# Moving three transposing transfers, one key part and two hand-over no-ops in a hand-written instruction order

## The chip, the core and the metric

The kernel runs on one core of a Trainium2 chip. Times are device microseconds (us) of one execution. Its engines are named as in the profile: PE (TensorE matmul; PEld is its weight load), DVE (VectorE), ACT (ScalarE), POOL (GpSimd) and SP (SyncE, which here only issues transfers). POOLq, SPq and so on are the instruction queues of these engines, in which waits and issues of transfers stand.

## The reference

One input `x` of 2048 tokens by 448 features feeds two branches, which are combined by a gate:

```python
xn = layernorm(x)
# A: attention over a dilated window, 16 heads of 28
idx = pos[:, None] - 2 * arange(8)[None, :]        # 8 keys, every second token back
logits = einsum("bhsd,bhswd->bhsw", q, k[idx]) * 28 ** -0.5   # masked where idx < 0
s = einsum("bhsw,bhswd->bhsd", softmax(logits), v[idx]) @ wo
# B: feed-forward 448 -> 1792 -> 448
f = gelu(xn @ w1 + b1) @ w2 + b2
return x + s * silu(f)
```

## The kernel before

**Tiling.** The even and the odd tokens are taken apart, since the window only reaches tokens of the same parity; the 2048 positions are then 16 tiles of 128, numbered 0 to 15, and four chunks of four tiles. The features lie on the partitions in three full groups of 128 and a rest of 64.

**Stages.** Each tile is normalised and transposed (`xnT`). Projections give queries and keys (`qk_rows`, evacuated by ACT or DVE to `qk_tok` or `qk_pair`, and transposed by a transfer on SP into `qkT`) and values (`vproj`, evacuated to `v_tok`, written by a transfer on POOL to a DRAM tensor `v_rows`, and read back shifted by other transfers on POOL into `v`, `values`). Attention works on nine blocks of 224 to 228 positions, 0 to 8, each in two halves. For a block, `keys` makes two masked copies of its keys, `kb` (part 0 and part 1, each of two instructions); `scores` multiplies keys and queries (L680); ACT takes the exponential into `E` (L686); DVE or POOL multiplies by the mask (L696); `values_sum` multiplies by the values (L711); DVE divides into a buffer `a` (L722, L727), of which there are three in turn; and two transfers per half, on POOL or SP, write `a` to a DRAM tensor `o_rows` (L734). `turn` reads two tiles of `o_rows` back transposed (transfers on SP into `xnT`, whose earlier content is spent, or `oT`) and `final_pair` or `final` projects them (L745, L760). The feed-forward branch is `ff1` (L554, evacuated by ACT, L558) and `ff2` (L580, L606). `store` multiplies by the gate, adds `x` and writes out (L780).

**Row pairs.** Most projections run as a `pair`: two products of 64 rows each side by side in the array. A pair has two parts on PE, and between them a no-op on some other engine (L437): it waits for the last matmuls of the first part, and the second part waits for it. POOL, SP or ACT may carry the no-op.

**What sets the order.** Nothing is scheduled by a cost: a string `ORDER` lists all 1033 steps, and each engine executes its own steps in that order. A letter gives the engine (P = PE, V = DVE, A = ACT, G = POOL, S = SP, D = the landing of a transfer, which costs nothing by itself) and the number the step. A step can wait for another engine, and what stands behind it on its engine then waits too. Banks of PSUM and buffers are handed out in the same order.

The steps that the change and the prediction speak of:

| step | what it is |
|---|---|
| S449, S426, S442 | transposes of queries and keys of tiles 15, 13 and 14 (L300, `qkT<-qk_tok`, `qkT<-qk_pair`) |
| S375 | the same for tile 11, ahead of them on SP |
| S930, S932 | read-back of output rows, tiles 4 and 5, and 6 and 7 (L300, `xnT<-o_rows`) |
| S790, S797, S829, G788 | writes of `a` to `o_rows` (L734) of blocks 4 and 5 |
| G386, G390, G388, G392 | reads of `v` for block 4 (L294): two of 63 rows, then two of 64 |
| P783, P792 | first and second half of `values_sum` of block 4 (L711) |
| V861, A862 | the two key parts of block 7 (L665 on DVE, L663 on ACT) |
| P863, P868 | scores of block 7 (L680) |
| A891, A892, P893 | key parts and scores of block 8 |
| P964, P975 | final projections that read what S930 brings (L745) |
| 539, 514 | no-ops between the parts of two `ff1` pairs: P538 to P540, and P513 to P515 |
| A52 | a load of ACT's function table for gelu (L340) |
| V824 | the `a` of block 5's second half (L727), which reuses the buffer that S790 and G788 empty |
| P523 | first part of an `ff1` pair, whose bank V824 frees |

Of the kernel before, what the change touches and what calls it, by code (L numbers as in the profile page):

```python
# [39 lines left out]
V592 V745 V747 P732 V602 P377 V733 A603 V734 P370 G378 V735 P379 V736 G371 P354 V599 G739 S737 D738 D740 A383 S928  # L40
D929 V771 A600 P753 G384 D385 P372 V754 G355 V380 P356 A373 V755 G381 D382 P428 A357 V772 A360 P444 G358 D359 V756
V757 G361 D362 P773 V374 S445 S758 D759 P446 G429 G760 D761 G386 D387 A774 V750 S375 D376 P778 A776 V447 P430 A779
V752 P421 V801 A781 P762 V775 A448 G422 G390 D391 P423 V763 A431 V764 S449 D450 P451 G388 D389 A434 V765 V766 P605
A425 V424 G452 S767 D768 G392 D393 V777 G394 D395 V802 G396 D397 V604 G432 D433 S426 D427 V601 G435 D436 P453 V780
G606 P437 V782 G769 D770 A457 V454 P803 G458 D459 V831 A438 P439 A804 G455 D456 V832 P783 A806 P607 G805 V784 A441
V785 V786 V787 G461 D462 G463 D464 V440 S790 G788 D789 D791 V807 S442 D443 G460 P808 V611 P538 A809 V608 A811 P792
S539 P813 V810 A52 G465 D466 P513 V793 V794 G467 D468 P540 V795 S514 V796 A609 P515 V814 G799 S797 D798 D800 V815 A542
S932 D933 S930 D931 P528 V816 A541 V817 P533 V812 A516 A529 G818 D819 V610 G820 D821 P822 A612 P530 V861 A534 G469
D470 A517 V823 P535 V824 G471 D472 A532 P508 V825 V826 A537 V613 P523 G827 D828 S829 D830 A531 G509 A536 P510 S524
A862 P518 P953 S519 A512 P525 G954 A511 S934 D935 P955 A526 P520 V956 A527 P942 V960 G957 A522 V961 P833 P838 A521  # L50
G943 S958 D959 P944 S962 D963 A53 P614 V945 V949 V950 A839 S951 D952 A841 V840 V946 A834 P863 V842 S947 D948 G615 P868
A836 V835 P616 A869 V837 A871 G870 A864 A866 V865 G872 A891 P843 V620 P623 G867 V844 V845 A621 V846 A892 V847 V617
G848 D849 V622 P852 G850 D851 A618 S624 P893 P625 V853 A894 V854 A896 V855 V856 V619 G857 D858 V895 G859 D860 V897
P548 V629 V626 P964 A630 G549 A627 V631 P898 G965 P975 A899 V628 A901 P966 V900 G976 A54 V902 P543 S936 D937 V971 P977
# [68 lines left out]
def kernel(  # L123
# [16 lines left out]
    NT = S // P  # L140
# [7 lines left out]
    TPC = CH // P  # L148
# [236 lines left out]
    def norm(t):  # L385
        def f1(k):
            nc.vector.tensor_scalar(buf(p_xn, k)[:, :D], x_sb[:, t, :], mv[:, t, 0:1], rstd[:, t:t + 1],  # L387
                                    op0=ALU.subtract, op1=ALU.mult)
        a = plan.add("DVE", f1, [t_rs[t]], take=(p_xn,))

        def f2(_):
            nc.vector.tensor_copy(buf(p_xn, a)[:, D:], buf(p_xn, a)[:, KF:D])
        twice = plan.add("DVE", f2, [a])
        if t >= TPC:
            t_xT[t] = dma_T(xnT[:, :, t * P:(t + 1) * P], lambda: buf(p_xn, a)[:], [twice], (p_xn, a, 0))
            return
        halves, apart = [], t < 2
        for i in range(2):
            def f3(k, i=i):
                xn, tp = buf(p_xn, a), half_bank(buf(p_b, k if apart else (halves or [k])[0]))  # L400
                for kt in (2 * i, 2 * i + 1):
                    nc.tensor.transpose(tp[:, kt, :], xn[:, kt * P:(kt + 1) * P], ident[:])
            halves.append(plan.add("PE", f3, [twice if i else a, t_ident] + halves, take=() if i and not apart else (p_b,), give=((p_xn, a, 0),) if i else ()))

        n = 2 if t < 2 else 4
        copied = []
        for k0 in range(0, KT, n):
            def f4(k, k0=k0, b=halves[k0 // 2 if apart else 0]):
                copy(k.on, xnT[:, k0:k0 + n, t * P:(t + 1) * P], half_bank(buf(p_b, b))[:, k0:k0 + n, :])
            b = halves[k0 // 2 if apart else 0]  # L410
            copied.append(plan.add(("DVE", "ACT"), f4, [halves[(k0 + n - 1) // 2]], give=((p_b, b, 0),)))
        t_xT01[t], t_xT[t] = copied[0], plan.add("DMA", None, copied)
# [38 lines left out]
    def first_batch(tiles, tiles0=0):  # L451

        f = []
        for kt in range(3):
            for i, js in enumerate(tiles):
                def f1(k, kt=kt, i=i, js=js):
                    for q, j in enumerate(js):
                        j.part(buf(p_b, f[i] if kt else k, q), kt, 2, kt == 0, False)
                f.append(plan.add("PE", f1, ([t_xT01[tiles0 + i]] if kt < 2 else js[0].deps[:1]) + t_w[kt] + f[i:i + 1] * (kt > 0) + f[:1] * (i > 0), take=() if kt else (p_b,) * len(js) ))
        every = [(i, q, j) for i, js in enumerate(tiles) for q, j in enumerate(js)]  # L460

        def f2(k):
            def part(i, q, half):
                return lambda: tiles[i][q].part(buf(p_b, f[i], q), 3, half, False, True)
            together([part(0, 0, 0), part(1, 0, 0), part(0, 2, 0)], [part(0, 1, 1), part(1, 1, 1), part(1, 2, 1)])
        tt = plan.add("PE", f2, f + t_w[3])
        for i, q, j in every:
            j.evac(tt, f[i], q)

    t_row, t_qk = [[] for _ in range(NT)], {}  # L470

    def qk_rows(t, which):
        cs = slice(t * P, (t + 1) * P)

        def part(ps, kt, half, start, stop):
            r = half_rows(half)
            w = w_in[r, kt, which * D:(which + 1) * D] if kt < 3 else w_in3[r, 0, :]
            return nc.tensor.matmul(ps[:, :D], xnT[r, kt, cs], w, start=start, stop=stop)  # L478

        def evac(a, own, i):  # L480
            b = qk_tok[qk_at[t]]
            free = t_qk.get(max([u for u in range(t) if qk_at[u] == qk_at[t]], default=None))

            def fn(k):
                copy(k.on, b[:, which, :, :DH], buf(p_b, own, i)[:, :D].rearrange("p (h c) -> p h c", h=H))
            t_row[t].append(plan.add(("ACT", "DVE"), fn, [a, t_qz[qk_at[t]], free], give=((p_b, own, i),)))
            if len(t_row[t]) == 2:
                t_qk[t] = dma_T(qkT[:, :, :, cs].rearrange("p w g c -> p (w g) c"), lambda: b[:].rearrange("p w h c -> p (w h c)"),
                                t_row[t], None)
        return _Job(D, part, [t_xT[t]] + t_w[0] + t_w[1] + t_w[2], evac, (), t_w[3])  # L490

    t_v, v_at, h_at = {}, {}, {}
    t_vt = {}

    def vproj(t):
        k0 = t * P

        def part(ps, kt, half, start, stop):
            r = half_rows(half)
            w = w_in[r, kt, 2 * D:] if kt < 3 else w_in3[r, 1, :]  # L500
            return nc.tensor.matmul(ps[:, :D], xnT[r, kt, k0:k0 + P], w, start=start, stop=stop)  # L501

        def evac(a, own, i):
            b = v_tok[t % len(v_tok)]

            def fn(k):
                copy(k.on, b[:, :, :DH].rearrange("p (e x) c -> p e x c", e=2),
                     buf(p_b, own, i)[:, :D].rearrange("p (x e c) -> p e x c", e=2, c=DH))
            d = plan.add(("ACT", "DVE"), fn, [a] + t_vw + [t_vt[u] for u in (t - len(v_tok),) if u >= 0], give=((p_b, own, i),))
            t_vt[t] = dma_sb(lambda k: v_rows[k0:k0 + P, :], lambda: b[:].rearrange("p h c -> p (h c)"), [d])[1]  # L510
        return _Job(D, part, [t_xT[t]] + t_w[0] + t_w[1] + t_w[2], evac, (), t_w[3])
# [313 lines left out]
    def project(c):  # L825
        for t in range(c * TPC, (c + 1) * TPC):
            norm(t)
        vs = [vproj(t) for t in range(c * TPC, (c + 1) * TPC)]
        for i, t in enumerate((c * TPC, c * TPC + 2)):
            js = [[qk_rows(u, w) for w in range(2)] for u in (t, t + 1)]  # L830
            if not c and not i:
                first_batch([js[n] + [vs[n]] for n in range(2)], t)
            else:
                for n in range(2):
                    pair(*js[n], c < 2)
                pair(vs[2 * i], vs[2 * i + 1], c < 2)
        if c == NCH - 1:
            done = [j for t in range(c * TPC, NT) for j in (t_qk[t], t_vt[t])]
            t = plan.add("POOL", None, done)
            t.slots[p_g] = list(range(4, 4 + len(late_g)))  # L840
            t.give = tuple((p_g, t, i) for i in range(len(late_g)))
        for b in blocks_of[c]:
            values(b)

    project(0)

    def f_b1(k):
        nc.tensor.transpose(half_bank(buf(p_b, k))[:, 0, :], b1r[:], ident[:])
    b1_at = plan.add("PE", f_b1, [t_b1r, t_ident], take=(p_b,))
    t_b1 = plan.add("DVE", lambda _: nc.vector.tensor_copy(b1[:], half_bank(buf(p_b, b1_at))[:, 0, :NMT]), [b1_at], give=((p_b, b1_at, 0),))  # L850

    project(1)

    turned = [t_xT[t].deps[0] for t in range(TPC, 2 * TPC)]
# [43 lines left out]
    t = plan.add("POOL", None, [seen[b, 1][0] for b in range(2)])  # L898
# [43 lines left out]
```

## Time and profile before

| | |
|---|---|
| median of three runs | 152.55 us |
| the three runs | 151.75, 152.55 and 156.65 us |
| the profiled execution, its own time | 151.89 us |
| its span, first to last instruction | 150.2 us |
| PE, busy share of the span | 144.2 us, 96% |
| DVE | 109.8 us, 73% |
| ACT | 88.3 us, 59% |
| POOL | 64.0 us, 43% |
| granted TensorE clock | 0.999 |

Between the span and the execution's own time lie 1.7 us before the first and behind the last instruction. A busy share is an average over the whole span; what an edit is worth is read from the stretch in which it lies, here the one from about 75 to 120 us after the start.

### The profile page before, as it was taken

How to read it: one execution, taken by the hardware profiler on the slowest of the kernel's cores; microseconds unless marked ns; L12 is line 12 of the kernel's file. 1: busy time of each engine (PE TensorE's matmuls, PEld its weight loads, DVE VectorE, ACT ScalarE, POOL GpSimd, SP SyncE). 2: the span in 40 equal slices, each digit the busy share in tenths (PEclk: the TensorE clock that was granted, in tenths of full speed). 3: DMA queues.
4: the chain of work that ended last, by engine and by line, in shares of the span. 5: the costliest groups of instructions: out<-in, count | busy, mean ns of one | idle time of the engine just before them, and what ended most of it. 6: DMA issues, size and time to landing. Idle time of an engine off the chain costs nothing.

```text
span 150.2 us, 4657 instructions
## 1 busy us (share of the span) xinstructions
PE 144.2 (96%) x1828; PEld 79.9 (53%) x1828; DVE 109.8 (73%) x295; ACT 88.3 (59%) x161; POOL 64.0 (43%) x120
## 2 busy tenths in 40 slices
PE   7999999999999999999999699999999999999991
PEld 2444555444455665565565365556666664455570
DVE  3889944197954899989999689808689997581642
ACT  3253576776683772744673519989883976571120
POOL 6733594004535585741468457902363024110200
PEclk9999999999999999999999999999999999999999
DMA  4999998999499969998399899795102332264202
GB/s 145 303 273 321 207 199 190 243 311 258 116 138 203 117 152 225 230 209 179 109 223 178 98 244 175 189 194 137 65 0 73 76 101 62 71 155 112 65 31 61
DMA packets 43966, 24.17 MB, mean 161 GB/s; under 512 B 33822, under 2 KB 42022, under 8 KB 43944
## 3 DMA queue, kind: packets, MB, share of 16 engines
q1 hardware_dynamic: 41080, 17.25, 59.8%
q0 software_dynamic: 2720, 6.51, 16.4%
q8 instruction: 14, 0.23, 0.6%
q10 hardware_dynamic: 144, 0.11, 0.3%
q14 instruction: 8, 0.07, 0.1%
HBM read 9.70 MB, written 6.29 MB: 106 GB/s over the span
## 4 chain that ended last, share of the span: by engine, by line
PE 79%; DVE 8%; DMA 7%; issue 2%; SPq 2%; ACT 1%; DVEq 0%; POOLq 0%
PE bank L554 28%; PE bank L580 14%; PE bank L478 9%; PE bank L606 7%; PE bank L745 6%; DMA v<-v_rows 5%; PE bank L501 5%; PE bank L264 3%; DMA o_rows<-a 3%; PE bank L680 2%; PE bank L711 2%; DVE a L727 2%; SPq L300 2%; PE bank L760 1%; DVE E L696 1%
## 5 line engine op out<-in xcount | busy, mean ns | idle before, releaser
L554 PE MATMUL bank<-xnT,w 64*128 64x512 bf16 x392 | 46.9, 376 | 0.0
L558 ACT ACTIVATE h<-bank,b 128x512 bf16<-128x512 f32 x56 | 35.1, 685 | 15.7 <-PE bank L554 15.2
L580 PE MATMUL bank<-w,h 64*128 64x448 bf16 x336 | 33.8, 349 | 0.0
L554 PEld LDWEIGHTS <-w 64*128 64x128 bf16 x392 | 20.8, 94 | 18.7 <-issue 0.7
L478 PE MATMUL bank<-w_in,xnT 64*128 64x448 bf16 (+1 forms) x212 | 26.4, 351 | 0.2 <-DVE xnT L251 0.2
L686 ACT ACTIVATE E<-bank 128x456 bf16<-128x456 f32 (+1 forms) x36 | 17.4, 551 | 11.9 <-PE bank L680 10.8
L580 PEld LDWEIGHTS <-h 64*128 64x128 bf16 x336 | 17.4, 94 | 12.7
L727 DVE TENSOR_TENSOR a<-bank,rd 114x448 bf16<-114x448 f32 (+1 forms) x36 | 22.3, 623 | 1.6 <-DMA o_rows<-a 0.6
L734 POOL DMA_DIRECT2D o_rows<-a x25 | 13.3, 534 | 21.2 <-DVE a L727 9.4
L294 POOL DMA_DIRECT2D v<-v_rows x22 | 13.9, 635 | 8.6 <-PE bank L478 2.9
L478 PEld LDWEIGHTS <-xnT 64*128 64x128 bf16 (+1 forms) x212 | 10.4, 94 | 9.3 <-DVE xnT L251 0.7
L353 DVE BATCH_NORM_STATS2 st<-x_sb 128x6 f32<-128x448 bf16 x16 | 9.4, 610 | 6.9 <-DMA x_sb<-in_A_x_dram 6.8
L501 PE MATMUL bank<-w_in,xnT 64*128 64x448 bf16 (+1 forms) x106 | 13.7, 349 | 0.0
L622 DVE TENSOR_TENSOR y<-bank,b 128x448 f32<-128x448 f32 x15 | 9.0, 619 | 6.3 <-PE bank L606 5.0
L294 POOL DMA_DIRECT2D v_rows<-v_tok x16 | 9.1, 572 | 8.0 <-DVE v_tok L251 4.5
L634 ACT ACTIVATE t<-y 128x448 f32<-128x448 f32 x12 | 6.9, 580 | 8.0 <-DVE y L622 8.0
L606 PE MATMUL bank<-w,h 128*128 128x448 bf16 (+2 forms) x70 | 11.4, 315 | 0.0
L665 DVE TENSOR_SCALAR kb<-qkT,plane 128x512 bf16<-128x512 bf16 x30 | 10.5, 403 | 1.2 <-DMA qkT<-qk_tok 1.2
L696 POOL TENSOR_TENSOR E<-E,m_gen 128x456 bf16<-128x456 bf16 x8 | 8.5, 1076 | 6.7 <-ACT E L686 6.7
L776 POOL TENSOR_TENSOR o<-x_sb,sg 128x448 bf16<-128x448 bf16 x3 | 3.1, 1030 | 18.0 <-DVE sg L770 9.3
L387 DVE TENSOR_SCALAR xn<-x_sb,mv,rstd 128x448 bf16<-128x448 bf16 x16 | 6.2, 394 | 5.7 <-DMA xnT<-xn 3.4
L696 DVE TENSOR_TENSOR E<-E,m_gen 128x456 bf16<-128x456 bf16 (+1 forms) x24 | 9.0, 391 | 1.4 <-ACT E L686 1.4
(83 smaller groups left out, 181.1 us busy)
## 6 DMA issues: line engine op xcount, KB each, us to landing
v_rows<-v_tok POOLq DMA_DIRECT2D x16, 128.0 KB, 3.7
v<-v_rows POOLq DMA_DIRECT2D x14, 128.0 KB, 3.8
out_dram<-o SPq DMA_DIRECT2D x15, 112.0 KB, 1.7
w<-in_B_w_dram SPq DMA_DIRECT2D x2, 784.0 KB
o_rows<-a POOLq DMA_DIRECT2D x23, 64.1 KB, 2.9
w<-in_B_w_dram SPq DMA_DIRECT2D x2, 672.0 KB
x_sb<-in_A_x_dram SPq DMA_DIRECT2D x3, 448.0 KB, 7.3
w_in<-in_A_wqkv_dram SPq DMA_DIRECT2D x3, 336.0 KB, 5.1
```

Of the source, the lines that this page charges most:

```text
L294: nc.gpsimd.dma_start(dst(k), src())
L478: return nc.tensor.matmul(ps[:, :D], xnT[r, kt, cs], w, start=start, stop=stop)
L501: return nc.tensor.matmul(ps[:, :D], xnT[r, kt, k0:k0 + P], w, start=start, stop=stop)
L554: return nc.tensor.matmul(ps[:], w1[r, kt, ms], xnT[r, kt, cs], start=start, stop=stop)
L558: nc.scalar.activation(buf(p_h, own, i)[:], buf(p_b, own, i)[:], ACT.Gelu_apprx_tanh, bias=b1[:, mt:mt + 1])
L580: return nc.tensor.matmul(ps[:, :D], buf(*h_at[(c, mt)])[r, j * P:(j + 1) * P], w2[r, mt, :], start=start, stop=stop)
L606: nc.tensor.matmul(ps[:, :n], buf(*h_at[(c, mt)])[:, j * P:(j + 1) * P], w2[:, mt, cs], start=(mt == 0 and not biased), stop=(mt == NMT - 1))
L665: nc.vector.tensor_scalar(dst, src, plane[:, e:e + 1], None, op0=ALU.mult)
L686: nc.scalar.activation(buf(p_E, k)[:, :n], buf(p_b, a, r)[:, :n], ACT.Exp, scale=SCALE)
L696: (nc.gpsimd if k.on == "POOL" else nc.vector).tensor_tensor(out=E, in0=E, in1=m, op=ALU.mult)
L727: nc.vector.tensor_tensor(out=o, in0=sums(k, e)[:, :, :, :DH], in1=buf(p_rd, rd)[rows].unsqueeze(2).unsqueeze(3).to_broadcast((2 * nq, 8, ...
L734: (nc.gpsimd if k.on == "POOL" else nc.sync).dma_start(o_rows[n + i * nq:n + i * nq + nq, :], buf(p_a, own)[i * nq:i * nq + nq, i, :])
```

## The change

Nothing is added to the work or taken from it. In `ORDER`, with the rest of the string in place:

- S449 (and its landing D450) goes from before the second value projection of tiles 12 and 13 to behind S932, where S930 stood.
- S426 (D427) goes from ahead of S790 to just behind it.
- S930 (D931) goes from behind S932 to behind four output writes.
- V861 goes from behind V610 and P822 to behind V613, five DVE steps later.
- The no-ops 539 and 514 are issued by ACT and not by SP: 539 in front of A52, 514 behind it.

The step G460 in `project` is a bookkeeping step without an instruction: it hands the memory of the input weights on to the gate's buffers. It listed the landing of the query and key transposes among what must stand ahead of it in the string; two of these now stand behind it, so it lists the evacuations instead.

```diff
-V752 P421 ... A434 V765 V766 P605 ... S449 D450 P451 ...
+V752 P421 ... P451 ...
-... G432 D433 S426 D427 V601 ...
+... G432 D433 V601 ...
-... S790 G788 D789 D791 ... P538 A809 V608 A811 P792
-S539 P813 ... V795 S514 V796 ... S932 D933 S930 D931 P528
+... S790 S426 D427 G788 D789 D791 ... P538 A809 V608 A811 A539 P792 P813
+... V795 A514 V796 ... S932 D933
+S449 D450 P528
-... P530 V861 A534 ... V613 P523
+... P530 A534 ... V613 V861 P523
-... S947 D948
+... S947 S930 D931 D948
@@
-            done = [j for t in range(c * TPC, NT) for j in (t_qk[t], t_vt[t])]
+            done = [j for t in range(c * TPC, NT) for j in t_row[t] + [t_vt[t]]]
```

On SP, in the second half of the program, the rows stood as follows. `qk_tok_153` belongs to tile 11 (S375), `qk_tok_151` to tile 15 (S449), the first `qk_pair` to tile 13 (S426), the second to tile 14 (S442); the two `xnT<-o_rows` are S932 and S930.

```order
L300 DMA_TRANSPOSE qkT<-qk_tok_153 128x8x128
L300 DMA_TRANSPOSE qkT<-qk_tok_151 128x8x128
L734 DMA o_rows<-a 57x576
L300 DMA_TRANSPOSE qkT<-qk_pair 128x8x128
L734 DMA o_rows<-a 56x576
L300 DMA_TRANSPOSE qkT<-qk_pair 128x8x128
L734 DMA o_rows<-a 56x576
L300 DMA_TRANSPOSE xnT<-o_rows 128x4x256 x2
L734 DMA o_rows<-a 57x576
L300 DMA_TRANSPOSE oT<-o_rows 128x4x256
```

In the changed program the same stretch of SP reads:

```order
L300 DMA_TRANSPOSE qkT<-qk_tok_153 128x8x128
L734 DMA o_rows<-a 57x576
L734 DMA o_rows<-a 56x576
L300 DMA_TRANSPOSE qkT<-qk_pair 128x8x128 x2
L734 DMA o_rows<-a 56x576
L300 DMA_TRANSPOSE xnT<-o_rows 128x4x256
L300 DMA_TRANSPOSE qkT<-qk_tok_151 128x8x128
L734 DMA o_rows<-a 57x576
L300 DMA_TRANSPOSE oT<-o_rows 128x4x256
```

Between tile 11's transpose and the write S790 (the `56x576` row that comes first) stood two transposes, and now stands none; tiles 13 and 14 follow S790 back to back; tile 15 has S930's old place. S930 itself comes four output writes later, outside these rows.

On ACT, around the table load that leads from the exponentials of block 5 to the gelus of `ff1`, the difference is (+ now, - before; `PE_49` is PE's semaphore):

```order
 L686 ACTIVATE E<-bank_157 128x456 [waits PE_49]
 L686 ACTIVATE E<-bank_158 128x456 [waits PE_49]
-L340 ACT_TABLE_LOAD
+L340 ACT_TABLE_LOAD [waits PE_49]
 L340 ACTIVATE sink<-eps_t 128x1
-L634 ACTIVATE t_107<-y_104 128x448 [waits DVE_49]
+L634 ACTIVATE t_107<-y_104 128x448 [waits PE_49,DVE_49]
 L558 ACTIVATE h_128<-bank_156,b_71 128x512 [waits PE_49]
```

The two new waits are those of the no-ops, which have no row of their own: the table load now waits for the first part of one `ff1` pair (P538), and the tanh behind it for that of another (P513).

On DVE the key part V861 (`kb_149`) moves behind block 5's last divisions and a gate step:

```order
 L696 TENSOR_TENSOR E<-E,m_gen 128x456
 L638 SCALAR_TENSOR_TENSOR qkT<-t_107,y_104 128x448
-L665 TENSOR_SCALAR kb_149<-qkT,plane 128x2x4x64 x2
 L722 RECIPROCAL rd_101<-bank_159 114x8
 L727 TENSOR_TENSOR a<-bank_159,rd_101 114x8x2x28
@@ -196,4 +195,5 @@
 L727 TENSOR_TENSOR a<-bank_157,rd_102 114x8x2x28
 L638 SCALAR_TENSOR_TENSOR qkT<-t_106,y_105 128x448
+L665 TENSOR_SCALAR kb_149<-qkT,plane 128x2x4x64 x2
 L770 SCALAR_TENSOR_TENSOR sg_112<-bank_161,g_108 128x448
```

Two reciprocals, two divisions and one gate step now stand ahead of it.

More of the change, by code (lines that the diff above doesn't have):

```diff
@@ L42 @@
 V757 G361 D362 P773 V374 S445 S758 D759 P446 G429 G760 D761 G386 D387 A774 V750 S375 D376 P778 A776 V447 P430 A779
[L43 to L51, printed above, removed]
+V752 P421 V801 A781 P762 V775 A448 G422 G390 D391 P423 V763 A431 V764 P451 G388 D389 A434 V765 V766 P605 A425 V424
+G452 S767 D768 G392 D393 V777 G394 D395 V802 G396 D397 V604 G432 D433 V601 G435 D436 P453 V780 G606 P437 V782 G769
+D770 A457 V454 P803 G458 D459 V831 A438 P439 A804 G455 D456 V832 P783 A806 P607 G805 V784 A441 V785 V786 V787 G461
+D462 G463 D464 V440 S790 S426 D427 G788 D789 D791 V807 S442 D443 G460 P808 V611 P538 A809 V608 A811 A539 P792 P813
+V810 A52 G465 D466 P513 V793 V794 G467 D468 P540 V795 A514 V796 A609 P515 V814 G799 S797 D798 D800 V815 A542 S932 D933
+S449 D450 P528 V816 A541 V817 P533 V812 A516 A529 G818 D819 V610 G820 D821 P822 A612 P530 A534 G469 D470 A517 V823
+P535 V824 G471 D472 A532 P508 V825 V826 A537 V613 V861 P523 G827 D828 S829 D830 A531 G509 A536 P510 S524 A862 P518
+P953 S519 A512 P525 G954 A511 S934 D935 P955 A526 P520 V956 A527 P942 V960 G957 A522 V961 P833 P838 A521 G943 S958
+D959 P944 S962 D963 A53 P614 V945 V949 V950 A839 S951 D952 A841 V840 V946 A834 P863 V842 S947 S930 D931 D948 G615 P868
 A836 V835 P616 A869 V837 A871 G870 A864 A866 V865 G872 A891 P843 V620 P623 G867 V844 V845 A621 V846 A892 V847 V617
```

## The prediction, on record before the result was known

> **What bounds the kernel now.** I read the page's busy shares and its 40 slices, then the chain of waits in order of time, then the timelines of PE and of SP's queue where the chain leaves PE.
>
> ```profile
> PE 144.2 (96%) x1828; PEld 79.9 (53%) x1828; DVE 109.8 (73%) x295; ACT 88.3 (59%) x161; POOL 64.0 (43%) x120
> PE   7999999999999999999999699999999999999991
> DMA  4999998999499969998399899795102332264202
> ```
>
> PE is busy 144.2 of 150.2 us. A slice is 3.76 us; apart from the two ends only one, the 23rd (82.6 to 86.4 us), falls below nine tenths. DMA is at eight or nine tenths from the 21st slice to the 25th (75 to 94 us) and nearly idle from the 29th on. In the chain of waits that one slice is the last place where PE waits for anything:
>
> ```profile
> 78.52 0.02 POOLq L437
> ...
> 79.14 7.00 DMA v<-v_rows
> ...
> 86.19 0.39 PE bank L711 x15
> ...
> 145.19 0.04 DVEq L768
> ```
>
> From 86.19 to 145.19 all its pieces are PE. So a stall that goes at 86 us moves the end by its full length, unless a new wait appears in those 59 us. The stall on PE's timeline:
>
> ```profile
> 84.75 0.19 PE L711 MATMUL bank<-v,E 64*128 64x58 bf16 x1
> 86.19 0.39 PE L711 MATMUL bank<-v,E 64*128 64x58 bf16 x15 [1.26 <-DMA v<-v_rows]
> ```
>
> P783 runs its first matmul, with the values of G386, and its second waits 1.26 us for those of G390, which POOL issued at 79.14 and which took 7.00 us to land. The other reads of `v` say whether that is normal (the transfers issued at 77.13, 79.14, 90.2 and 92.7 us, with their time to landing at the end of the row):
>
> ```profile
> v<-v_rows POOLq DMA_DIRECT2D x1, 63.0 KB, 5.2
> ...
> v<-v_rows POOLq DMA_DIRECT2D x1, 63.0 KB, 7.0
> ...
> v<-v_rows POOLq DMA_DIRECT2D x1, 128.0 KB, 3.9
> ...
> v<-v_rows POOLq DMA_DIRECT2D x1, 128.0 KB, 3.0
> ```
>
> Reads twice as large land in 3.0 to 3.9 us later on. What is different at 79 us stands in SP's queue:
>
> ```profile
> 76.62 3.26 SPq L300 DMA_TRANSPOSE qkT<-qk_tok  x2
> ...
> 80.96 1.23 SPq L300 DMA_TRANSPOSE qkT<-qk_pair  x1
> 88.34 0.32 SPq L734 DMA_DIRECT2D o_rows<-a  x1
> 88.91 1.23 SPq L300 DMA_TRANSPOSE qkT<-qk_pair  x1
> ...
> 95.05 2.58 SPq L300 DMA_TRANSPOSE xnT<-o_rows  x2
> ...
> 103.23 3.24 SPq L780 DMA_DIRECT2D out_dram<-o  x4
> ```
>
> Three transposes are issued from 76.62 to 82.19: S375, S449 (the second of the first row), S426. SP's queue takes 83.0% of the 16 DMA engines' time between 78.6 and 86.2 us, and 55.8% between 90 and 99:
>
> ```profile
> q1 hardware_dynamic: 2692, 0.74, 83.0%
> ...
> q1 hardware_dynamic: 2242, 0.64, 55.8%
> ```
>
> **The change part by part.** *S449 and S426 leave the stretch of the stall.* Only S375 then shares the engines with G390. PE asks for it at 84.94 (84.75 + 0.19), so the stall goes whole if it lands within 5.8 us of its issue at 79.14. The nearest row is G386, the same size, issued 2 us earlier and half a microsecond behind S375: 5.2 us, though S449 was issued beside it at about 78.6 and S426 at 80.96. Without these two G390 should take no longer than that. At 5.2 us it lands at 84.3 and the whole 1.26 us go; at the 3.0 us of the late reads too, with 2.8 us to spare; at 7.0 us nothing goes. I take 1.26, since 1.2 of 7.0 us have to be found and two of the three transposes that ran beside it are gone. Upper bound: the weight load's own idle time, 1.5 us.
>
> ```profile
> PEld L711 <- DMA v<-v_rows: 1.5, 1, 1.5
> POOL v_rows L294 <- DMA v<-v_rows: 2.5, 1, 2.5
> ```
>
> The second row is what is late next: POOL waited 2.5 us for the same reads before it could write values of tiles 14 and 15. That wait hangs on what comes earlier, and so do DVE's divisions behind P783, so both engines move forward with PE. P792 needs G388 and G392, which share the relief.
>
> *S426 and S442 follow S790.* S790 waits for DVE, not for SP; at its 88.34 it is issued, S426 then takes 1.23 us and S442 is issued at some 90.0 and not 88.91, or at 88.8 when all stands 1.26 earlier. Their readers:
>
> ```profile
> 97.89 1.33 ACT L663 ACTIVATE kb<-qkT,plane 128x512 bf16<-128x512 bf16 x2
> ...
> 106.25 0.63 PE L680 MATMUL bank<-qkT,kb 64*128 64x57 bf16 x32
> ...
> 108.69 1.35 ACT L663 ACTIVATE kb<-qkT,plane 128x512 bf16<-128x512 bf16 x2
> ...
> 116.16 0.35 PE L745 MATMUL bank<-wo,xnT 64*128 64x448 bf16 x1
> ...
> qkT<-qk_tok SPq DMA_TRANSPOSE x10, 5.7
> ...
> xnT<-o_rows SPq DMA_TRANSPOSE x4, 5.4
> ```
>
> Landing in 5.7 us (the longer of the two medians of such transposes), S442 issued at 90.0 is there at 95.7, 2.2 us before A862 (97.89). Cost 0. V861's two instructions now run after V613, at about 97; their reader P863 starts at 106.25, nine microseconds later. V861 no longer stands in front of V823. Cost 0, gain 0, since no PE step in the chain waits there now.
>
> *S449 to 96.4* (where S930 stood) lands at about 102; A891 reads it at 108.69. *S930 behind the four output writes* is issued at 106.5 (103.23 + 3.24) and lands at 111.9; P964 reads it at 116.16, so 4 us are left, on DMA engines that stand at one to three tenths. S936 and the next outputs are queued behind it on SP, but come more than 10 us later. Cost 0 for both.
>
> *The no-ops on ACT.* A hand-over costs 0.02 us by the row of POOLq above. What counts is when ACT comes to it:
>
> ```profile
> 89.47 0.99 ACT L686 ACTIVATE E<-bank 128x456 bf16<-128x456 f32 x2 [3.74 <-PE bank L680]
> 90.48 1.28 ACT L340 ACT_TABLE_LOAD   x1
> 91.77 0.20 ACT L340 ACTIVATE sink<-eps_t 128x1 f32<-128x1 f32 x1
> ...
> 90.75 3.88 PE bank L554 x36
> ```
>
> 539 stands behind the two exponentials, at 90.46, and P540 begins after 8 of the 36 matmuls (0.108 us each), at 91.6: hidden. 514 stands behind the table load, at 91.97; P515 begins after 14, at 92.26: 0.3 us in hand. ACT's work there starts when PE's scores (P808) are done, so both move together. Cost 0, bound 0.3 either way round. Left on SP, 539 would have stood behind two transposes' issue, until about 91.3; ACT avoids that.
>
> Sum against the profiled execution: 151.89 - 1.26 = 150.63 us. That execution lies 0.66 below the median of the three runs and 0.14 above the fastest, so I take a third of the way to the median: 150.9 us.
>
> **The rivals.**
>
> *A. No change: the reads are not slowed by the transposes.* Then G390 would have been late because GpSimd prepared it slowly beside a busy VectorE.
>
> ```profile
> 78.60:82.40 3.80, 3.80 (x50) 1.96 (x44) 3.73 (x11) 1.52 (x4) 3.02 (x5) 1.00 1.28 184
> 90.00:94.00 4.00, 4.00 (x68) 2.34 (x66) 3.86 (x11) 3.97 (x8) 3.13 (x6) 1.00 1.19 167
> ```
>
> DVE (the third busy column) worked 3.73 of 3.80 us there, which speaks for it; but it worked 3.86 of 4.00 us from 90 to 94, and those reads landed in 3.0 and 3.9 us. The Trainium skill, "SBUF — State Buffer", section "SBUF: two separate sides", states this as a rule: VectorE in a two-port mode locks GpSimd out, and a transfer issued from GpSimd then only appears slow. By that rule the stall would stay; the later reads disagree. The stall stays, and with it the median: 152.2 us, between the fastest two runs. Chance 0.17.
>
> *B. Slower: the jam moves to the writes of `a`.* S426 and S442 now run exactly when S790 and G788 empty the buffer that V824 refills.
>
> ```profile
> 91.49 0.55 POOL L734 DMA_DIRECT2D o_rows<-a  x1
> ...
> 95.32 0.62 DVE L727 TENSOR_TENSOR a<-bank,rd 114x448 bf16<-114x448 f32 x1
> ...
> 94.86 4.53 PE bank L554 x42
> ...
> o_rows<-a POOLq DMA_DIRECT2D x1, 63.0 KB, 3.5
> ```
>
> G788 landed at 95.0, V824 began at 95.32 and ended at 95.94, and P523 took its bank after 20 of the 42 matmuls, at 97.02. So 0.3 + 1.1 = 1.4 us of delay are free. Should the write take the 7.0 us of G390, it is 3.5 late and PE loses 2.1: against the gain of 1.26 that is 0.8 slower, 153.4 us on the median's scale. PE loses from a landing of 4.9 us on (3.5 + 1.4), the kernel from 6.2 (the gain on top), and more than 2% from 9.2 (another 3.05). Against it: before, S442 ran there already and G788 took only 3.5, and the reads ahead of G788 on POOL come earlier too. Chance 0.13.
>
> *C. More than the stall goes.* The three runs spread over 4.9 us, which one trace can't explain; if a longer wait at P783 is what the slow one shows, the change takes it away as well, and the median gains 3 us or more, to 149.4. Nothing in this profile shows such a wait: PE's idle time in it is 6 us in all, most of it at the two ends. Chance 0.12.
>
> **How the numbers follow.** My forecast, a gain of 0.6 to 1.6 us, has the rest, 0.58. The range: below, the fastest run less the upper bound, 151.75 - 1.5 = 150.25, less 0.45 for runs that differ by chance (about half of the 0.8 between the two near ones): 149.8. Above, rival A on the median plus the no-ops' bound, 152.55 + 0.3, rounded to 152.9. Left out are most of C and of B. Two per cent, 3 us, is about what a measurement of this kernel tells from no change. The forecast and A lie within it, and so does B at 153.4. Faster by over 2%: C and a little of the forecast, 0.14. Slower by over 2%: B at its far end, and surprises, 0.12. Within: 0.74.
>
> **What would show it.** In the changed kernel's profile P783's 16 matmuls should stand in one row without a wait for `v`; G390 should land in 4 to 5.5 us; the 23rd slice of PE should read 9; the first L745 of P964 should come about 1.3 us earlier than 116.16. A wait of PE at P523, or of DVE for `o_rows` at V824, would show rival B; a wait of a weight load for ACT at P515, the no-ops' cost; G390 again near 7 us, rival A. The prediction is wrong if P783's wait goes and the span does not fall: then one of the waits counted as hidden was not.

## The result, and the profile after

The changed kernel takes 151.06 us (median of 20 runs, 149.73 to 154.44) against 152.95 us of the kernel before (20 runs, 151.62 to 156.65). The ratio is 0.9866, with a 95% interval of 0.9828 to 0.9904: a gain of 1.3%, below the 2% that the forecast counted as faster. Ratios here and below leave out runs that stand over 1.5% above the fastest of their kernel; medians and ranges are of all runs and stand alone for the first four kernels below, where one of 17 runs of the kernel before would be left. The profiled execution takes 150.40 us (span 148.7) against 151.89 (150.2) before, 1.49 us less.

From the page of the changed kernel, the busy times and the slices of PE and DMA:

```profile
PE 143.8 (97%) x1828; PEld 76.7 (52%) x1828; DVE 111.5 (75%) x295; ACT 88.3 (59%) x161; POOL 64.1 (43%) x120
...
PE   7999999999999999999999999999999999999991
...
DMA  4999999999698959996399669965612332275012
```

The one slice of PE that stood at 6, the 23rd, now reads 9. Its busy time did not change (144.2 before): only a hole in it closed. DMA falls from 8 and 9 to 6 and 6 in the 23rd and 24th slice, and rises from 1 to 6 in the 29th, where S930 is now.

PE's timeline of the changed kernel (start, length, what, how many) where the stall had been:

```profile
84.68 0.38 PE L711 MATMUL bank<-v,E 64*128 64x58 bf16 x16
84.90 2.81 PE L580 MATMUL bank<-w,h 64*128 64x448 bf16 x28
```

P783's 16 matmuls stand in one row with no wait, and the products behind them start at 84.90 where they started at 86.40. The read G390 by itself, its line's instructions in the changed kernel (length and time of issue, then time to landing):

```profile
L294 POOL DMA_DIRECT2D v<-v_rows x1: 739/739/739, 79.1 to 79.1; - x1
...
DMA to landing us min/median/max: 5.1/5.1/5.1
```

It is issued at the same 79.1 us and lands after 5.1 us, not 7.0. The chain of waits of the changed kernel from there to the end (start, length, what):

```profile
84.84 0.22 PE bank L711 x16
...
114.82 0.76 PE bank L745 x8
...
143.11 0.58 PE bank L760 x4
143.69 0.03 DVEq L768
```

All of it is PE, as before, and every piece comes 1.5 us earlier: P964's first product at 114.82 (116.34 in the chain before), the last one at 143.11 (144.60). So the time was won at one place and nothing of it was given back in the 59 us behind it. SP's timeline of the changed kernel shows the cost of the crowding, which did not reach PE:

```profile
76.56 1.24 SPq L300 DMA_TRANSPOSE qkT<-qk_tok  x1
80.33 6.82 SPq L734 DMA_DIRECT2D o_rows<-a  x2
87.25 3.94 SPq L300 DMA_TRANSPOSE qkT<-qk_pair  x2
91.28 0.51 SPq L734 DMA_DIRECT2D o_rows<-a  x1
92.96 1.24 SPq L300 DMA_TRANSPOSE xnT<-o_rows  x1
94.26 1.45 SPq L300 DMA_TRANSPOSE qkT<-qk_tok  x1
...
100.67 1.23 SPq L300 DMA_TRANSPOSE oT<-o_rows  x1
101.95 3.01 SPq L780 DMA_DIRECT2D out_dram<-o  x4
105.01 1.24 SPq L300 DMA_TRANSPOSE xnT<-o_rows  x1
```

S426 and S442 together hold SP for 3.94 us (1.23 each was assumed). The row at 100.67 is S934, the read-back for the final projection of another pair of tiles; it stands ahead of the four output writes and will matter below.

### The profile page after: what moved, and what is told of

Same layout as the page of the kernel before. It is cut to its first block, busy times and chain, and to the rows that moved or that the text cites. A ratio compares the mean times of both kernels' runs of the same rounds, so it can differ in the third digit from the quotient of the medians.

```text
span 148.7 us, 4655 instructions
## 1 busy us (share of the span) xinstructions
PE 143.8 (97%) x1828; PEld 76.7 (52%) x1828; DVE 111.5 (75%) x295; ACT 88.3 (59%) x161; POOL 64.1 (43%) x120
## 4 chain that ended last, share of the span: by engine, by line
PE 68%; DVE 19%; DMA 7%; issue 3%; POOL 1%; DVEq 0%; SPq 0%; POOLq 0%
PE bank L554 25%; PE bank L580 11%; PE bank L478 7%; PE bank L606 7%; PE bank L745 6%; PE bank L501 4%; DMA xnT<-xn 4%; DMA o_rows<-a 3%; PE bank L264 3%; DVE a L727 3%; DVE kb L665 3%; DVE xn L392 2%; PE bank L711 2%; DVE g L638 2%; DVE xn L387 2%
## 5 line engine op out<-in xcount | busy, mean ns | idle before, releaser
L554 PEld LDWEIGHTS <-w 64*128 64x128 bf16 x392 | 19.5, 94 | 19.9 <-issue 0.7
L580 PEld LDWEIGHTS <-h 64*128 64x128 bf16 x336 | 16.0, 94 | 14.0
```

The source lines that it names most:

```text
L554: return nc.tensor.matmul(ps[:], w1[r, kt, ms], xnT[r, kt, cs], start=start, stop=stop)
L580: return nc.tensor.matmul(ps[:, :D], buf(*h_at[(c, mt)])[r, j * P:(j + 1) * P], w2[r, mt, :], start=start, stop=stop)
```

## The experiments

T stands for the prediction's account: the traffic of the two moved transposes made G390 late, and the other three moves cost and bring nothing. The rivals are that G390 was late for another reason (the prediction's A), and that the other moves carry a part of the time; narrower forms of both came with the second and third set of runs and are stated there. Each kernel is compared with runs of the kernel before on the same chip; the three sets of experiments ran on three chips, so times of different sets are not compared closely. In the diffs, G460's line of bookkeeping goes with every kernel in which S449 or S426 moves.

### Tile 15's transpose alone

```diff
-... V764 S449 D450 P451 ...
+... V764 P451 ...
-... S932 D933 S930 D931 P528
+... S932 D933 S930 D931 S449 D450 P528
```

> The kernel before with one step moved: the transpose of tile 15 goes behind both read-backs of output rows; tile 13's transpose, the no-ops on SP, V861 and the read-back of tiles 4 and 5 stay. Theory T (the traffic of the two transposes slows the read G390): with one of the two away G390 lands in 5 to 6 us and not 7.0, the wait at P783 falls from 1.4 us to 0 to 0.4, and the kernel is 1.0 to 1.5 us faster than before. Rival A (GpSimd is slow beside VectorE, whatever SP does): the wait stays, 0 us. Rival N (the gain came from the no-ops' change of queue or from V861 and S930): 0 us.

Measured: 151.35 us (median of 6, 150.2 to 151.96) against 153.37 (17 runs: the fastest 150.12, all others 152.43 or more). G390 lands after 5.4 us and the wait at P783 is gone, with S426 still in its old place:

```profile
84.92 0.38 PE L711 MATMUL bank<-v,E 64*128 64x58 bf16 x16
```

PE's and SP's timelines of this kernel show what came instead. First PE (in brackets the wait ahead and its releaser):

```profile
100.01 0.82 PE L554 MATMUL bank<-xnT,w 64*128 64x512 bf16 x6 [1.14 <-SPq L437]
```

Then SP:

```profile
93.63 2.58 SPq L300 DMA_TRANSPOSE xnT<-o_rows  x2
96.27 3.14 SPq L300 DMA_TRANSPOSE qkT<-qk_tok  x1
99.45 0.44 SPq L734 DMA_DIRECT2D o_rows<-a  x1
```

Three transposes stand back to back on SP, and issuing the third took 3.14 us. A write and a no-op between two parts of an `ff1` pair are queued behind it, so PE waited 1.14 us for SP. That execution took 151.96 us, no less than the 151.89 of the profile before: the 1.14 us, with another wait of 0.50 us at 36.41 us, far ahead of the moved step, took up what was won at P783. So tile 15's transpose is enough for the stall, but the place that it goes to is not free while S930 stands there too.

### Tile 13's transpose, with the no-ops

```diff
-... D433 S426 D427 V601 ... S790 G788 ... A811 P792
-S539 P813 ... V795 S514 V796
+... D433 V601 ... S790 S426 D427 G788 ... A811 A539 P792
+P813 ... V795 A514 V796
```

> The kernel before with the transpose of tile 13 behind S790 and both no-ops on ACT; tile 15's transpose, V861 and the read-back of tiles 4 and 5 stay. Theory T: tile 15's transpose still runs beside G390, so it lands in about 6 us: the wait falls to 0.2 to 0.8 us and the kernel is 0.6 to 1.2 us faster than before. Rival A: 0 us. Rival N for the no-ops: the whole gain, 1.5 us.

Measured: 153.56 us (median of 12, 152.2 to 156.35) against 153.37; no gain to be seen, where T had 0.6 to 1.2 us. From 75 us on, PE's timeline of this kernel has two waits (another, of 0.78 us, stands at 36.76 us, far ahead of the moved steps):

```profile
86.79 0.39 PE L711 MATMUL bank<-v,E 64*128 64x58 bf16 x15 [0.79 <-DMA v<-v_rows]
...
98.80 2.76 PE L554 MATMUL bank<-xnT,w 64*128 64x512 bf16 x22 [1.18 <-DVE a L727]
```

The wait for `v` stays, at 0.79 us; G390 took 6.5 us. The second is rival B's place, P523 waiting for the `a` that frees its bank, but not by rival B's way. DVE's timeline of the same kernel:

```profile
97.62 0.35 DVE L665 TENSOR_SCALAR kb<-qkT,plane 128x512 bf16<-128x512 bf16 x1 [1.54 <-DMA qkT<-qk_pair]
97.89 0.20 DVE L722 RECIPROCAL rd<-bank 114x8 f32<-114x8 f32 x1
98.12 0.62 DVE L727 TENSOR_TENSOR a<-bank,rd 114x448 bf16<-114x448 f32 x1
```

V861, the key part, stands in its old place here. Its second instruction waits 1.54 us for tile 14's transpose, which SP issues later because S426 now stands ahead of it; the division behind it in DVE's order waits too.

### The rest alone: S930, V861 and the no-ops

```diff
-... A811 P792 S539 P813 ... V795 S514 V796 ... S932 D933 S930 D931 P528
+... A811 A539 P792 P813 ... V795 A514 V796 ... S932 D933 P528
-... P530 V861 A534 ... V613 P523 ... S947 D948
+... P530 A534 ... V613 V861 P523 ... S947 S930 D931 D948
```

> The other half of the change alone: the read-back of tiles 4 and 5 behind the output writes, V861 behind V613, both no-ops on ACT; the transposes of tiles 13 and 15 where they were. Theory T: the wait at P783 stays at 1.3 to 1.5 us and the time stays within 0.3 us of before. Rival N: 1 us or more faster.

Measured: 152.11 us (median of 6, 150.79 to 155.6) against 153.37, where T had no change. In PE's timeline the wait is there as before:

```profile
85.51 0.39 PE L711 MATMUL bank<-v,E 64*128 64x58 bf16 x15 [1.05 <-DMA v<-v_rows]
```

The reads landed in 6.8 to 7.1 us, and the profiled execution took 151.84 us, against 151.89 before. The trace agrees with T. Over all runs the mean is 152.67 us against 153.59, 0.6% less, with ranges that overlap: whether these moves bring some tenths of a microsecond stays open, and no row of the profile shows such a gain.

### The no-ops back on SP

The changed kernel with only this undone:

```diff
-... A811 A539 P792 P813 ... V795 A514 V796
+... A811 P792 S539 P813 ... V795 S514 V796
```

> The changed kernel with the no-ops 539 and 514 back on SP, where they stood. Theory T with the queue argument: 539 stands behind the issue of the transposes of tiles 13 and 14, which ended at 91.2 in the changed kernel's profile, and P540 wants to begin at 90.1: PE waits about 1.1 us there and the kernel is 0.8 to 1.2 us slower than the changed one (so 0.3 to 0.7 faster than before). If SP's queue is not held by a transpose that it has issued: no difference from the changed kernel.

Measured: 151.37 us (median of 6, 150.88 to 152.82) against 153.37. PE's timeline:

```profile
91.11 3.20 PE L554 MATMUL bank<-xnT,w 64*128 64x512 bf16 x28 [1.34 <-SPq L437]
```

PE waits 1.34 us for the no-op, because S426 and S442 hold SP for 4.08 us in front of it. The profiled execution took 151.59 us, 1.2 more than the changed kernel's 150.40.

### Two moves and nothing else

After the first set the account was narrower: tile 15's transpose is the cause, S930 has to leave the place that it goes to, and the other moves only pay for moving tile 13's. So, in the kernel before:

```diff
-... V764 S449 D450 P451 ... S932 D933 S930 D931 P528 ... S947 D948
+... V764 P451 ... S932 D933 S449 D450 P528 ... S947 S930 D931 D948
```

> The kernel before with two steps moved: the transpose of tile 15 to the place of the read-back of tiles 4 and 5, and that read-back behind the four output writes, as in the change. Tile 13's transpose, V861 and the no-ops on SP stay. Theory T2 (tile 15's transpose alone makes the wait at P783, the rest of the change only pays for moving tile 13's): no wait at P783, no wait for SP at the no-ops 524 and 519 (1.14 us where the read-back was left in place), so a span of 148.5 to 149.2 and a time equal to the changed kernel's within 0.4 us. Theory T1 (both transposes have to go): a wait of 0.3 us or more at P783 is left.

Measured: 150.53 us (median of 6, 149.76 to 152.45) against 153.17, ratio 0.9847 (0.9787 to 0.9907); the profiled execution took 149.76 us and PE waits nowhere between the start and the tail. G390 landed after 5.7 us, later than the 5.1 of the whole change, and a weight load waited 0.3 us for it. Once S449 is moved, S426's move buys half a microsecond of slack, and no time that these runs show.

### The changed kernel with S930 left in its old place

```diff
-... S932 D933 S449 D450 P528 ... S947 S930 D931 D948
+... S932 D933 S930 D931 S449 D450 P528 ... S947 D948
```

> The changed kernel with the read-back of tiles 4 and 5 left where it was, ahead of tile 15's transpose. Theory Q (a third transpose on SP is issued only when an earlier one has made room, and the no-op 524 stands behind it): PE waits 0.8 to 1.5 us for SP at P525, the span is 149.5 to 150.2. If the read-back's move is free: as the changed kernel, 148.7.

Measured: 151.32 us (median of 4, 149.67 to 153.31); the ratio, 0.9811 (0.9729 to 0.9893), rests on the two shortest of them. PE's timeline of the profiled execution, of 153.31 us:

```profile
101.35 0.82 PE L554 MATMUL bank<-xnT,w 64*128 64x512 bf16 x6 [2.69 <-SPq L437]
```

And SP's:

```profile
93.01 5.37 SPq L300 DMA_TRANSPOSE xnT<-o_rows  x2
98.43 2.31 SPq L300 DMA_TRANSPOSE qkT<-qk_tok  x1
```

Three transposes held SP for 7.7 us, and PE lost 2.69, where 0.8 to 1.5 were expected. Two of the four runs (149.67 and 150.08 us) leave no room for such a loss, so S930's move takes away a wait that some executions have and others don't.

### The changed kernel with V861 left in its old place

```diff
-... P530 A534 ... V613 V861 P523
+... P530 V861 A534 ... V613 P523
```

> The changed kernel with V861 left where it was, ahead of block 5's last divisions. Theory Q2 (V861 waits for tile 14's transpose, which now comes behind tile 13's, and the divisions that free P523's bank stand behind it): DVE waits 1 to 2 us for the transposes there, PE 0.7 to 1.3 us at P523, the span is 149.4 to 150.0. If V861's move is free, as my prediction has it: 148.7.

Measured: 151.98 us (median of 4, 151.15 to 152.54), ratio to the kernel before 0.9945 (0.9883 to 1.0007). PE's timeline:

```profile
95.87 2.76 PE L554 MATMUL bank<-xnT,w 64*128 64x512 bf16 x22 [0.84 <-DVE a L727]
```

P523 waits 0.84 us, by the same way as in the kernel with tile 13's move: the key part waits for `qk_pair` and holds the division. The profiled execution is 0.75 us longer than the changed kernel's (151.15 against 150.40).

### G390 issued earlier as well

The changed kernel, with G390 straight behind G386 and so ahead of a no-op on POOL:

```diff
-... G386 D387 A774 ... G422 G390 D391 P423 ...
+... G386 D387 G390 D391 A774 ... G422 P423 ...
```

> The changed kernel with the read G390 issued right behind G386, ahead of a no-op on POOL. G390 is issued 0.7 to 1.3 us earlier and lands by 83.5; P783 has no wait to lose any more, so the profile's span stays at 148.7, within 0.2. If in other executions of the changed kernel this read still comes late, the runs' median falls by 0.3 us or more.

Measured: 150.89 us (median of 6, 149.73 to 152.22), ratio 0.986 (0.9804 to 0.9915): nothing beyond the change's 0.9866, as must be where G390 is no longer waited for. The profile is of the longest run, 152.22 us, and shows what made this run long. Its chain of waits:

```profile
94.69 7.77 DMA o_rows<-a
102.46 0.02 issue
102.48 1.23 SPq L300
103.71 0.05 issue
103.76 4.29 DMA out_dram<-o
108.05 0.02 issue
108.07 0.62 DVE o L776
108.69 0.93 DVE E L696 x3
```

And PE's timeline behind it:

```profile
109.36 0.67 PE L711 MATMUL bank<-v,E 64*128 64x58 bf16 x16 [2.05 <-DVE E L696]
```

A write to `o_rows` took 7.77 us. S934, which reads those rows back, waits for it on SP and starts at 102.48 (100.67 in the changed kernel's profile). The output writes are queued behind S934; DVE waits for one of them, since it needs the output buffer that the write empties; the masks behind that are late, and PE waits 2.05 us. From this came the theory S: the spread of the runs is S934's place on SP, not a longer wait at P783.

### The output writes ahead of S934

The changed kernel, with S934 behind the four output writes and S930:

```diff
-... A511 S934 D935 P955 ... S947 S930 D931 D948
+... A511 P955 ... S947 S930 D931 S934 D935 D948
```

> The changed kernel with one more step moved: the read-back of tiles 8 and 9 (S934), which waits on SP for the writes of output rows, goes behind the four output writes and the read-back of tiles 4 and 5. Theory S (in the longer executions of the changed kernel a late write of output rows holds S934, the output writes queued behind it on SP hold DVE, and PE waits 2 us for a mask): the profile's span stays at 148.7 or a little under, no wait of DVE for the output writes, and the runs lie together: most of them at 150.5 or below, none above 152, a median of 150.0 to 150.5, 0.5 us or more under the changed kernel's 151.06. If the longer executions come from something else: the same spread up to 153 to 154 and a median of about 151.

Measured: 149.90 us (median of 6, 149.57 to 150.67) against 153.72, ratio 0.9879 (0.9824 to 0.9935). SP's timeline:

```profile
101.33 3.23 SPq L780 DMA_DIRECT2D out_dram<-o  x4
104.65 1.24 SPq L300 DMA_TRANSPOSE xnT<-o_rows  x1
106.07 1.92 SPq L300 DMA_TRANSPOSE oT<-o_rows  x1
```

The writes go at 101.33, without a wait for a landing ahead of them, and PE has no wait in the profile. The six runs lie within 1.1 us, where the changed kernel's 20 spread over 4.7. All six are below 150.7 us, while 10 of those 20 are above 151.4; with the changed kernel's even odds six such in a row would come once in 64 times. The changed kernel itself was not run on this chip, but the kernel before spread over 4.4 us there. The ratio is no better than the change's; what went are long runs, which it does not count. By the medians this is the best version: it is 1.2 us below the changed kernel's and 3.8 below that of the kernel before on the same chip.

### Other traffic in the transposes' old places

The changed kernel, with two copies of 256 KB from the core's own memory (SBUF) to itself, issued by SP where S449 and S426 had stood (an addition whose data nobody reads). One kernel copies 128 rows of 2 KB each, the other the same bytes in 1024 pieces of 256 bytes. VectorE's and GpSimd's work is the changed kernel's in both.

```diff
-... V764 P451 ... D433 V601 ...
+... V764 S1033 D1034 P451 ... D433 S1035 D1036 V601 ...
+scratch = sb("scratch", [P, 2, 1024])
+for i in range(2):
+    dma("SP", scratch[:, i, :], w1[:, 0, 0:1024])
```

The kernel with the small pieces differs in the last lines:

```diff
+scratch = sb("scratch", [P, 2, 8, 130])
+for i in range(2):
+    dma("SP", scratch[:, i, :, :128], w1[:, 0, 0:1024].rearrange("p (a b) -> p a b", a=8))
```

> The changed kernel with two plain transfers added on SP, from SBUF to SBUF, 256 KB each in rows of 2 KB, where the transposes of tiles 15 and 13 stood before. VectorE's and GpSimd's work is that of the changed kernel. Theory T by bytes: they slow G390 as the transposes did, to about 7 us, and the wait at P783 is back at 1 to 1.5 us. Theory T by packets (a transpose is some 1000 small packets, these are 128 large ones): G390 lands in 5 to 5.8 us and there is no wait. Rival A: no wait either.

> The same two added transfers, 256 KB each, but written in pieces of 256 bytes (1024 each). Theory T by packets: G390 lands in 6.5 us or later and the wait at P783 is 0.7 us or more. Rival A: no wait, as in the changed kernel.

Measured: 149.8 and 152.21 us in rows of 2 KB; 152.56 and 153.63 us in small pieces, ratio of the latter to the kernel before 1.0085 (0.9971 to 1.0199). The transfers between 78.6 and 84.6 us, first in the changed kernel without copies (queue: packets, MB, share of 16 engines; `q1` is SP's; then landing of the 64 KB reads of `v`, G388 and G392):

```profile
q1 hardware_dynamic: 948, 0.28, 29.0%
...
v<-v_rows POOLq DMA_DIRECT2D x2, 64.0 KB, 4.3
```

The same view with rows of 2 KB:

```profile
q1 hardware_dynamic: 993, 0.74, 70.7%
...
v<-v_rows POOLq DMA_DIRECT2D x2, 64.0 KB, 5.3
```

With small pieces:

```profile
q1 hardware_dynamic: 2387, 0.65, 93.1%
...
v<-v_rows POOLq DMA_DIRECT2D x2, 64.0 KB, 6.5
```

And the kernel before in that stretch:

```profile
q1 hardware_dynamic: 2127, 0.55, 73.4%
...
v<-v_rows POOLq DMA_DIRECT2D x2, 64.0 KB, 6.6
```

G390 itself landed after 5.1, 5.8, 7.0 and 7.0 us in these four kernels. So the copies in rows of 2 KB cost it 0.7 us, and the same copies in small pieces 1.9 us, as much as the transposes had. PE's timeline of the kernel with small pieces has the old stall back (line numbers are one higher in this kernel):

```profile
85.63 0.39 PE L712 MATMUL bank<-v,E 64*128 64x58 bf16 x15 [1.29 <-DMA v<-v_rows]
```

With rows of 2 KB PE has no such wait, though a weight load waits 0.4 us. So small packets delay the read far more than the same bytes in large ones, and the large ones are not free either. No single count puts all kernels in order: with tile 15's transpose alone moved SP's queue holds 1714 packets and 0.49 MB in this stretch, in the kernel of two moves 1516 and 0.43 MB, both at some 70% of the engines, and G390 landed after 5.4 and 5.7 us. The small pieces also lie 260 bytes apart where they are written, which was not tried by itself.

### G390 earlier, in the kernel before

```diff
-... G386 D387 A774 ... G422 G390 D391 P423 ...
+... G386 D387 G390 D391 A774 ... G422 P423 ...
```

> The kernel before with nothing moved but the read G390, which is issued right behind G386 and ahead of a no-op on POOL, 1.2 us earlier; the transposes stay. If the wait at P783 is the time at which this read lands, it falls by 0.7 to 1.2 us (to 0.2 to 0.7) and the span to 149.0 to 149.6. If the wait has another cause: 150.2.

Measured: 155.69 us (median of 4: 149.93, 154.12, 157.26 and 157.72), inconclusive as a time. In the profile, of the run of 154.12 us, the wait at P783 is gone, and two others of half a microsecond or more stand in PE's timeline:

```profile
89.58 0.39 PE L711 MATMUL bank<-v,E 64*128 64x58 bf16 x15 [0.51 <-DMA v<-v_rows]
...
111.29 0.67 PE L711 MATMUL bank<-v,E 64*128 64x58 bf16 x16 [2.55 <-DVE E L696]
```

The first is P792, whose own reads are late now: two transposes' traffic is still there, and an earlier issue only hands the delay on. The second is S934's way again; SP came to S934 at 104.61 us in this run.

## Why the prediction was right, step by step

**The stall and its cause: shown.** The wait at P783 was the landing of G390, slowed by the transposes' traffic. It went with tile 15's transpose alone, stayed when everything but the transposes was moved, and came back with other small packets in their place. The forecast landing, no longer than G386's 5.2 us, came out at 5.1; part of that is luck, since G386 itself took 5.7 us in the changed kernel, and 5.8 was the limit. The prediction counted both transposes as one; tile 15's is enough, and tile 13's move then brings slack and no time. Without tile 15's it does not remove the wait: 0.79 us of it stayed.

**The step that was mis-sized: "the whole 1.26 us".** The profile gained 1.49 us. PE's idle time before a row is counted from the modelled end of the row before; but the row of one matmul is 0.19 us long, and the next one starts 0.014 us behind its start when nothing is missing (16 take 0.22 us in the chain). From start to start the stall cost 86.19 - 84.75 = 1.44 us. The rest, some 0.05, was there ahead of it already: P783 starts at 84.68, not 84.75. The ratio's interval, 1.0 to 1.7% of 152.95 us, is 1.5 to 2.6 us; the profile's gain is its near end. The medians differ by 1.89 us, more than the forecast's 0.6 to 1.6. That 150.9 us stands so near to the measured 151.06 is in part luck: the term of the stall was too small, and the kernel before also came out 0.4 us higher in 20 runs than in the three from which the forecast started. What the medians gained beyond the profile's 1.49 us is not explained.

**"S426 and S442 follow S790 ... Cost 0": right for PE, not for SP.** Issue took 3.94 us and not 2.5, and S442's data came late enough to stop V861 where it had stood: with V861 unmoved, the transposes were there at 94.69 us and A862 started at 95.93 in that execution, 1.2 us in hand where 2.2 were forecast.

**"V861 ... gain 0, since no PE step in the chain waits there now": wrong.** The reason looked at the kernel before, in which S442 was issued early. With S426 ahead of S442 the old place costs 0.84 us on PE (1.18 in the kernel with tile 13's move). The move is part of the price of S426's, and without S426's move it is not needed, as the kernel of two moves shows.

**S930: "Cost 0 for both" right, its worth missed.** The prediction asked what S930's new place costs, and not what its old place would cost once S449 stood behind it: 1.14 us in one kernel's profile, 2.69 in another's.

**The no-ops: right.** The prediction had SP's no-op late behind two transposes and ACT as the way round; on SP it costs 1.34 us, on ACT nothing.

**Rival A falls.** GpSimd's and VectorE's work is the same in the two kernels with copies, and the stall comes with the small pieces only. The Trainium skill's rule in "SBUF — State Buffer", section "SBUF: two separate sides", did not decide here: it would have kept the stall in all of these kernels. Another of its rules bears on the copies: "DMA: Bandwidth & Descriptors", section "Why small descriptors are slow (HBM only)", says that transfers from SBUF to SBUF do not suffer the penalty for small pieces. Here both copies are such transfers, and SP's queue, with the copies and all else in it, took 93.1% of the engines' time for 0.65 MB with small pieces against 70.7% for 0.74 MB with rows of 2 KB, half as much again per byte, beside the longer delay of the other queue; for these copies the measurement decides.

**Rival B had the right place and the wrong way.** P523's bank was at stake, through the key part on DVE, not through the write of `a`. The change's own move of V861 keeps it away.

**Rival C: the spread does not come from P783.** The changed kernel has lost the wait, and its 20 runs still spread over 4.7 us, against 5.0 before. The profiles of two long executions, both of kernels in which G390 is issued early, have no wait at P783, but S934 held on SP by a late write; with S934 moved, the runs lay within 1.1 us. That this makes every long run is not shown: the two longest of the changed kernel, 154.27 and 154.44 us, had a granted clock of 0.989, against 0.996 to 1.000 in the other 18, and no long run of the changed kernel or of the kernel before was profiled.

## What to carry to other kernels

Price a stall from start to start on the critical engine, not by the idle time beside it. When a step moves, ask of each companion move what its old place would cost after the main move, and not what it costs today; an undo of each part shows which moves pay and which only pay for another. On an in-order queue, put what waits for a landing behind what frees a buffer.

## What the runs showed of the hardware that was not expected

- The issue of a transpose on SP takes 1.23 to 1.25 us in many rows, but with others shortly before it, it held SP for 3.14 us, 5.37 for two, or 3.94 to 4.08 for two, and the no-ops and writes behind it waited. Two others in a row took 2.58 us, hardly more than twice 1.23, and one transpose 2.50 us, 3 us behind the one before (S426 in the kernel of two moves); no run shows what decides it.
- Two copies of 256 KB in pieces of 256 bytes in one queue delayed another queue's read from 5.1 to 7.0 us; the same bytes in rows of 2 KB delayed it to 5.8.
- The write to `o_rows` for which S934 waits landed after 5.3 us in one execution (issued at 95.4, S934 at 100.67) and after 7.77 in another (S934 at 102.48); the granted clock was 1.000 in both, and PE lost 2.05 us in the second.
